# A short block's first product moved behind the full block's first nine products, into another bank, and its copies into other buffers

## The chip, the cores and the metric

The kernel runs on one core of a Trainium2 chip. The metric is the device time of one execution in microseconds (us). An execution holds a linear attention with a recurrent state, a two-layer feed-forward with a leaky activation, and a mixture of eight experts with top-1 routing. The change touches only the experts, the last third of the program.

## The reference, cut to what matters

```python
def _moe2_ref(x, w_gate, w1, w2, capacity):      # x: 1536 x 384, E = 8 experts, F = 1024, capacity 384
    logits = x @ w_gate
    expert_idx = np.argmax(logits, axis=1)
    ...                                          # softmax weight gate_w of the chosen expert
    for i in range(N):                           # tokens go to their expert's list in order
        e = expert_idx[i]
        if counts[e] < capacity:
            disp[e, counts[e]] = x[i]; pos[i] = counts[e]; counts[e] += 1; keep[i] = True
    h = np.maximum(np.einsum('ecd,edf->ecf', disp, w1), 0.0)
    y = np.einsum('ecf,efd->ecd', h, w2)
    for i in range(N):
        if keep[i]: out[i] = gate_w[i] * y[expert_idx[i], pos[i]]
```

With the inputs of these runs the eight experts get 478, 132, 159, 141, 398, 57, 118 and 53 tokens; the first and the fifth are cut to 384.

## The kernel before, in words

Each expert takes its tokens in blocks of 128 rows. The first 128 rows of expert 0 are done earlier, ahead of the loop over experts, so the loop gives expert 0 two full blocks, expert 4 three, and experts 5, 6 and 7 one each. Experts 1, 2 and 3 have more than 128 and at most 160 tokens: they get one full block and a **short block** of up to 32 rows, which is computed beside the full one.

`expert` (line 903) reads the expert's count into a register on every engine (line 1212) and branches (line 923): where the count is marked as "one full and one short", `front(Short(e))` runs, otherwise `front()`. Then, in both cases, the weights of expert e + 2 are loaded through the SP queue (lines 396 and 399 for the two layers, line 654 for the token rows), and `rest()` runs. A further branch (line 934) starts more full blocks where the count asks for them. At the end of a branch that was not taken, each engine brings the semaphores to the values that the branch would have left (the EVENT_SEMAPHORE rows of line 934).

The full block works with split operands (a high and a low part, three products for each true one). `hidden(q, n0, n1)` (line 788) issues products n0 to n1 of the nine that make half q of the hidden layer, into a bank of pool `h`; `relu` (line 793) reads it on ScalarE (ACT); `turn` (line 798) transposes it into a bank of pool `att`, and its second step copies it to `gh` (ACT, line 804) and `gl` (VectorE, line 805). `second` (line 813) multiplies with the second weights into a bank of pool `acc`, and `put` (lines 696, 697) scales the result into `y` on VectorE and scatters its rows to the output with an indirect DMA from GpSimd (POOL). `also(n)` runs work for the next expert beside this one: the casts of its weights on ACT (line 687) with their low parts on VectorE or POOL (line 690), and the transposes of its tokens (line 668).

The short block uses unsplit weights with four groups of 32 rows in parallel: `few.hidden` (`eh_s`, line 869), `few.relu` (`hs_s`, line 875), `few.turn` (`pht_s`, line 881, copied to `hT_s` on VectorE, line 883), `few.second` (`ey_s`, line 892, copied to `part` on ACT, line 896), `few.gather` (`es`, line 900, scaled into `y_s` and scattered).

The order on every engine is the order in which the code is written. Tiles of one tag rotate through the tag's buffers in that order, and also those of branches that are not taken count. PSUM has four banks of pool `acc`, two of `h`, two of `att`. In SBUF the tag `cv` has two buffers: before the change `hs_s`, `hT_s`, `part`, `y` of the first block and `y` of the third share them. Tag `x2T` has one buffer (`y_s`, and `y` of a second block), tag `gl` three.

In `acc` an expert takes eight banks in turn, so `eh_s` of one expert gets the bank in which the expert before had its first block's `ey`, and must wait until VectorE has read that (line 696). In `cv` an expert takes five buffers, so `hT_s` gets the one that held `y` of the expert before, and must wait until its scatter has landed.

Of the kernel before, what the change touches and what calls it, by code (L numbers as in the profile page):

```python
# [8 lines left out]
F32 = mybir.dt.float32  # L9
# [9 lines left out]
P = 128  # L19
# [4 lines left out]
def kernel(  # L24
# [19 lines left out]
    NT, DM = out.shape  # L44
# [17 lines left out]
    HF = F2 // 2  # L62
# [6 lines left out]
    p1 = ctx.enter_context(tc.tile_pool(name="p1", bufs=1))  # L69
    p2 = ctx.enter_context(tc.tile_pool(name="p2", bufs=2))  # L70
    p3 = ctx.enter_context(tc.tile_pool(name="p3", bufs=3))
# [7 lines left out]
    def bank(name, where="att"):  # L79
        pool = {"att": ps_a, "h": ps_h, "acc": ps_acc}[where]  # L80
        return pool.tile([P, 512], F32, tag=where, name=name)
# [202 lines left out]
    def turn(i):  # L284
        t = tiles[i]
        t.turn_r()
        t.turn_k()
# [26 lines left out]
    def finished(i):  # L314
        tiles[i].put_x()


    PHASES = ((ahead, None, (-2, 1, 5, 9)), (turn, turned, (0, 3, 6, 9)), (score0, None, (2, 5, 8, 11)),
              (score1, None, (3, 5, 7, 10)), (output, None, (4, 7, 9, 14)), (finish, finished, (5, 8, 13, 14)))
    ROUTE_AT = ((2, 4, 7, 10, 12, 13, 14),) * (NBLK - 2) + ((2, 3, 4, 5, 6, 7, 8),)  # L320
# [82 lines left out]
    def exp_w(e, q):  # L403
        t = wsl[("e", e, q)]
        c = DC if q < 2 else HF // P
        return [t[:, x * PIECE:(x + 1) * PIECE].rearrange("p (c f) -> p c f", c=c) for x in range(2)]
# [285 lines left out]
    def put(rows, b, acc, name, n=P):  # L692

        pool, tag = ((p2, "cv"), (p1, "x2T"))[b % 2]
        y = pool.tile([P, DM], F32, tag=tag, name=f"y{name}")
        nc.vector.tensor_scalar(y[0:n], acc[0:n], rows[0:n, b, DM:DM + 1], None, op0=ALU.mult)
        ins = nc.gpsimd.indirect_dma_start(out, bass.IndirectOffsetOnAxis(rows[0:n, b, DM + 1:DM + 2].bitcast(I32), 0), y[0:n],  # L697
                                           None, bounds_check=NT - 1, oob_is_err=False)
        for old in puts:
            tc.declare_no_dep(ins.ins, old.ins, reason="each row has one token")  # L700
        puts.append(ins)

    class Early:
# [26 lines left out]
        def hidden(self, q, n0, n1):  # L730
            if n0 == 0:
                self.ph[q] = bank(f"eh_f{q}", "h")
            for n in range(n0, n1):
                (x, y), c = PASS[n // DC], n % DC
                nc.tensor.matmul(self.ph[q], self.d[x][:, c, :], exp_w(0, q)[y][:, c, :],
                                 start=(n == 0), stop=(n == 3 * DC - 1))
# [34 lines left out]
    def expert_block(e, b, beside):  # L771


        nm = f"{e}_{b}"
        d = [t[:, :, b * P:(b + 1) * P] for t in dT[e]]
        ph = [bank(f"eh{nm}_{q}", "h") for q in range(2)]
        h = {0: p2.tile([P, HF], F32, tag="ng", name=f"hs{nm}_0")}
        hT = {0: [p3.tile([P, HF], F32R, tag=t, name=f"{t}{nm}_0") for t in ("gh", "gl")]}

        def also(n):  # L780
            for f in beside.get(n, ()):
                f()

        def hidden(q, n0, n1):
            ww = exp_w(e, q)
            for n in range(n0, n1):
                (x, y), c = PASS[n // DC], n % DC
                nc.tensor.matmul(ph[q], d[x][:, c, :], ww[y][:, c, :], start=(n == 0), stop=(n == 3 * DC - 1))  # L788

        def relu(q):  # L790
            if q not in h:
                h[q] = p2.tile([P, HF], F32, tag="ng", name=f"hs{nm}_{q}")
            nc.scalar.activation(h[q], ph[q], AF.Relu)

        def turn(q):
            pt = bank(f"pht{nm}_{q}")
            for c in range(HF // P):
                nc.tensor.transpose(pt[:, c * P:(c + 1) * P], h[q][:, c * P:(c + 1) * P], ident)  # L798
            if q not in hT:
                hT[q] = [p3.tile([P, HF], F32R, tag=t, name=f"{t}{nm}_{q}") for t in ("gh", "gl")]  # L800
            hh, hl = hT[q]

            def f():
                nc.scalar.copy(hh, pt)  # L804
                nc.vector.tensor_tensor(hl, pt, hh.bitcast(F32), ALU.subtract)  # L805
            return f

        def second(py, q, low, cs=range(HF // P)):
            ww = exp_w(e, 2 + q)
            for c in cs:  # L810
                for x, y in PASS:
                    if (x == 1) == low:
                        nc.tensor.matmul(py, hT[q][x][:, c * P:(c + 1) * P], ww[y][:, c, :],  # L813
                                         start=(q == 0 and not low and c == 0 and y == 0),
                                         stop=(q == 1 and low and c == HF // P - 1))

        def front(few=None):

            if few:
                few.hidden()  # L820
            hidden(0, 0, 3 * DC)
            if few:
                few.relu()
            also(0)
            relu(0)
            if few:
                few.turn()
            hidden(1, 0, 5)
            put_h0 = turn(0)
            if few:  # L830
                few.second()
            also(1)
            put_h0()
            hidden(1, 5, 3 * DC)
            if few:
                few.gather()

        def rest():
            also(2)
            relu(1)  # L840
            also(3)
            py = ps_acc.tile([P, DM], F32, tag="acc", name=f"ey{nm}")
            second(py, 0, False, range(3))
            put_h1 = turn(1)
            put_h1()
            second(py, 0, False, range(3, HF // P))
            second(py, 0, True)
            also(4)
            second(py, 1, False)
            second(py, 1, True)  # L850
            put(dsp[e], b, py, nm)

        return front, rest

    class Short:
# [6 lines left out]
        def hidden(self):  # L862

            n = F2 // NCT
            self.ph = bank(f"eh{self.e}_s", "acc")
            for c in range(DC):
                for j in range(NCT):
                    q, o = j * n // HF, j * n % HF
                    nc.tensor.matmul(self.ph[j * CW:(j + 1) * CW, 0:n], dS[self.e][:, c, :], self.w[q][:, c, o:o + n],
                                     start=(c == 0), stop=(c == DC - 1), skip_group_check=True)  # L870
# [6 lines left out]
        def turn(self):  # L877
            n = F2 // NCT
            pt = bank(f"pht{self.e}_s")
            for c in range(n // P):  # L880
                nc.tensor.transpose(pt[:, c * P:(c + 1) * P], self.h[:, c * P:(c + 1) * P], ident)
            self.hT = p2.tile([P, DM], F32, tag="cv", name=f"hT{self.e}_s")[:, 0:n]
            nc.vector.tensor_copy(self.hT, pt[:, 0:n])

        def second(self):

            n = F2 // NCT // P
            self.pp = bank(f"ey{self.e}_s", "acc")
            for c in range(n):
                for j in range(NCT):  # L890
                    k = j * n + c
                    nc.tensor.matmul(self.pp[j * CW:(j + 1) * CW, 0:DM], self.hT[:, c * P + j * CW:c * P + (j + 1) * CW],
                                     self.w[2 + k * P // HF][:, k % (HF // P), :],
                                     start=(c == 0), stop=(c == n - 1), skip_group_check=True)
            self.part = p2.tile([P, DM], F32, tag="cv", name=f"part{self.e}")
            nc.scalar.copy(self.part, self.pp[:, 0:DM])

        def gather(self):
# [44 lines left out]
    with tc.manual_schedule():  # L943
# [43 lines left out]
        for n in range(7):  # L987
            m = 1 << n
            f = wpow[:, :, n:n + 1].to_broadcast([P, NP, m])
# [168 lines left out]
        g, n = NBLK * NFT - 1, SIZES[-1]  # L1158
# [85 lines left out]
```

## Time and profile before

| what | value |
|---|---|
| three timed runs | 464.07, 465.22, 461.83 us (median 464.07) |
| profiled execution | 462.03 us |
| its span, first to last instruction | 459.9 us |
| mean granted TensorE clock | 0.983 of full speed |
| TensorE (PE) busy | 424.0 us, 92% of the span |
| VectorE, ScalarE, GpSimd busy | 58%, 44%, 35% |
| experts 1, 2, 3 on PE (end of the expert before to own end) | 15.35, 20.15, 16.86 us |

The profile was taken in one execution; times inside it are us from the start of the span. A row of a timeline gives start, duration, engine, line, operation, output and inputs, and in brackets how long the engine was idle before it and what ended that. Rows of the same kind that follow each other are merged (x9). PE rows count each float32 product twice, since it is done in two passes: 12 products of `eh_s` appear as x24. A name with q behind an engine (PEldq, DVEq) is that engine's sequencer, which handles branches and semaphores. The experts lie between 316.9 and 455 us of the span.

### The profile page before, as it was taken

The page shows a single profiled execution, that of the slowest core. Times are in us where ns is not written, and L with a number is a line of the kernel's source. Part 1 is how long each engine was busy: PE and PEld are TensorE (multiplying, and loading weights), DVE is VectorE, ACT ScalarE, POOL GpSimd, SP SyncE. Part 2 cuts the span into 40 slices and gives each one's busy share as a digit, 9 for nine tenths or more (in the row PEclk, how much of TensorE's full clock was granted, in tenths as well). Part 3 has the DMA queues.
Part 4 walks back from the last instruction along what each step waited for, and adds up shares of the span by engine and source line. Part 5 has one row for each costly group of instructions (what it writes and reads, how often), then busy time and mean ns, then how long its engine had stood idle before and what let it go on. Part 6 is the DMA issues. An engine that isn't in the chain of part 4 may idle for free. (4 is left out here: it accounts for less than half of the span.)

```text
span 459.9 us, 7878 instructions
## 1 busy us (share of the span) xinstructions
PE 424.0 (92%) x3012; PEld 363.5 (79%) x3012; DVE 267.9 (58%) x475; ACT 201.7 (44%) x335; POOL 160.0 (35%) x141
## 2 busy tenths in 40 slices
PE   8877989699899999999999999999998887899985
PEld 7765778488788988988898889987966465798774
DVE  6888998999753444345433575354535355443651
ACT  1236545354444333323254444334636366543861
POOL 7845467454440231100300040031407145521660
PEclk9998999989999999999999999999999899899999
DMA  7989950649610105200900020016748728901900
GB/s 130 231 250 280 337 149 3 169 145 358 205 36 17 38 16 201 92 0 6 340 1 1 0 75 12 1 45 192 285 148 281 261 62 298 323 34 41 323 16 19
DMA packets 70513, 62.36 MB, mean 136 GB/s; under 512 B 41837, under 2 KB 58131, under 8 KB 70464
## 3 DMA queue, kind: packets, MB, share of 16 engines
q1 hardware_dynamic: 68832, 57.29, 40.4%
q0 software_dynamic: 1632, 4.40, 2.5%
q8 instruction: 32, 0.52, 0.5%
q14 instruction: 17, 0.14, 0.1%
HBM read 49.99 MB, written 12.18 MB: 135 GB/s over the span
## 5 line engine op out<-in xcount | busy, mean ns | idle before, releaser
L593 PE MATMUL acc<-wm,gh 128*128 128x384 f32 x384 | 100.8, 343 | 0.5 <-POOL wm L372 0.5
L608 PE MATMUL h<-xh,wm 128*128 128x512 f32 (+1 forms) x294 | 87.4, 407 | 3.6 <-DVE gl L631 3.6
L627 DVE SCALAR_TENSOR_TENSOR h<-ng,sign,h 128x512 f32<-128x512 f32 x48 | 36.1, 752 | 67.9 <-ACT ng L624 67.9
L593 PEld LDWEIGHTS acc<-wm,gh 128*128 128x128 f32 x384 | 68.8, 188 | 4.9 <-POOL wm L372 1.1
L593 PE MATMUL acc<-wm,gl 128*128 128x384 f32 x192 | 64.8, 338 | 0.0
L608 PEld LDWEIGHTS h<-xh,wm 128*128 128x128 f32 x294 | 53.2, 192 | 13.3 <-issue 2.9
L788 PE MATMUL eh<-we,d 128*128 128x512 f32 x198 | 54.5, 420 | 5.4 <-ACT we L687 3.1
L690 POOL TENSOR_TENSOR we<-re,we 128x768 fp32r<-128x768 f32 x21 | 41.7, 1984 | 50.8 <-ACT we L687 36.0
L624 ACT ACTIVATE ng<-h,slope 128x512 f32<-128x512 f32 x48 | 33.1, 690 | 57.3 <-PE h L608 57.3
L628 ACT CAST gh<-h 128x512 fp32r<-128x512 f32 x48 | 28.1, 586 | 63.3 <-DVE h L627 63.3
L687 ACT CAST we<-re 128x768 fp32r<-128x768 f32 x64 | 50.6, 839 | 1.8 <-ACTq L934 1.4
L690 DVE TENSOR_TENSOR we<-re,we 128x768 fp32r<-128x768 f32 x43 | 40.7, 973 | 17.8 <-ACT we L687 16.8
L788 PEld LDWEIGHTS eh<-we,d 128*128 128x128 f32 x198 | 37.2, 197 | 17.3 <-issue 9.9
L372 POOL TENSOR_TENSOR wm<-rm,wm 128x768 fp32r<-128x768 f32 x16 | 32.2, 2012 | 46.8 <-ACT wm L371 42.9
L526 POOL DMA_INDIRECT disp<-rows,sl x12 | 12.6, 1048 | 100.0 <-DVE run L552 64.4
L608 PE MATMUL h<-xl,wm 128*128 128x512 f32 (+1 forms) x147 | 42.9, 401 | 0.0
L631 DVE TENSOR_TENSOR gl<-h,gh 128x512 fp32r<-128x512 f32 x48 | 33.0, 687 | 15.6 <-ACT gh L628 15.0
L805 DVE TENSOR_TENSOR gl<-pht,gh 128x512 fp32r<-128x512 f32 x22 | 15.2, 692 | 44.1 <-ACT gh L804 42.4
L813 PE MATMUL ey<-we,gh 128*128 128x384 f32 x176 | 37.7, 346 | 0.0
L593 PEld LDWEIGHTS acc<-wm,gl 128*128 128x128 f32 x192 | 36.1, 188 | 0.0
L608 PEld LDWEIGHTS h<-xl,wm 128*128 128x128 f32 x147 | 28.2, 194 | 6.9 <-DVE xl L274 0.2
L813 PEld LDWEIGHTS ey<-we,gh 128*128 128x128 f32 x176 | 29.7, 189 | 0.4 <-ACT gh L804 0.4
(200 smaller groups left out, 612.8 us busy)
## 6 DMA issues: line engine op xcount, KB each, us to landing
re<-in_moe_w_dram SPq DMA_DIRECT2D x32, 768.0 KB, 6.6
rm<-in_moe_w_in_dram SPq DMA_DIRECT2D x8, 768.0 KB, 5.9
rm<-in_moe_w_out_dram SPq DMA_DIRECT2D x8, 768.0 KB, 6.7
disp<-rowss SPq DMA_DIRECT2D x1, 4825.0 KB
drow<-disp SPq DMA_DIRECT2D x7, 579.0 KB, 8.2
out_dram<-rowss SPq DMA_DIRECT2D x1, 2304.0 KB, 22.7
kn<-in_k_dram SPq DMA_DIRECT2D x10, 192.0 KB, 7.6
rn<-in_r_dram SPq DMA_DIRECT2D x10, 192.0 KB, 3.6
```

The source lines that it names most:

```text
L372: eng.tensor_tensor(lo, low.bitcast(F32), hi.bitcast(F32), ALU.subtract)
L593: nc.tensor.matmul(accs[(blk, s)], gs[g][a][:, s * P:(s + 1) * P], wout[b][:, ft % 2, :], start=(ft == 0 and n == 0), stop=(ft == NFT - 1 ...
L608: nc.tensor.matmul(phs[g][:, cols[0]:cols[1]], win[a][:, c, o:o + P], xs[b][:, c, cols[0]:cols[1]], start=(n == 0), stop=(n == 3 * DC - 1))
L624: nc.scalar.activation(ng, ph, AF.Relu, scale=slope[:, ft:ft + 1])
L627: nc.vector.scalar_tensor_tensor(ph, ng, sign[:, ft:ft + 1], ph, op0=ALU.mult, op1=ALU.add)
L628: nc.scalar.copy(gh, ph)
L631: nc.vector.tensor_tensor(gl, ph, gh.bitcast(F32), ALU.subtract)
L687: nc.scalar.copy(t[:, sl], src[:, sl])
L690: le.tensor_tensor(t[:, sl2], src[:, sl], t[:, sl].bitcast(F32), ALU.subtract)
L788: nc.tensor.matmul(ph[q], d[x][:, c, :], ww[y][:, c, :], start=(n == 0), stop=(n == 3 * DC - 1))
L805: nc.vector.tensor_tensor(hl, pt, hh.bitcast(F32), ALU.subtract)
L813: nc.tensor.matmul(py, hT[q][x][:, c * P:(c + 1) * P], ww[y][:, c, :], start=(q == 0 and not low and c == 0 and y == 0), stop=(q == 1 and ...
```

## The change

In a short expert the full block's first nine products, `also(0)` and the full block's `relu(0)` come first; then the short block's first product and its relu; then five products of the full block's second half; then both transposes. `eh_s` lies in a bank of pool `att` instead of `acc`, `hT_s` in the buffer of tag `x2T` and `part` in a buffer of tag `gl`, both instead of `cv`. The copy to `part` comes behind `also(1)` and the copies of the full block's first half. The branch for experts without a short block keeps its order.

```diff
         def front(few=None):
-            if few:
-                few.hidden()
             hidden(0, 0, 3 * DC)
-            if few:
-                few.relu()
             also(0)
             relu(0)
             if few:
+                few.hidden()
+                few.relu()
+            hidden(1, 0, 5)
+            if few:
                 few.turn()
-            hidden(1, 0, 5)
             put_h0 = turn(0)
             if few:
                 few.second()
             also(1)
             put_h0()
+            if few:
+                few.copy()
             hidden(1, 5, 3 * DC)
             if few:
                 few.gather()
...
-            self.ph = bank(f"eh{self.e}_s", "acc")
+            self.ph = bank(f"eh{self.e}_s")
...
-            self.hT = p2.tile([P, DM], F32, tag="cv", name=f"hT{self.e}_s")[:, 0:n]
+            self.hT = p1.tile([P, DM], F32, tag="x2T", name=f"hT{self.e}_s")[:, 0:n]
...
-            self.part = p2.tile([P, DM], F32, tag="cv", name=f"part{self.e}")
+
+        def copy(self):
+            self.part = p3.tile([P, HF], F32, tag="gl", name=f"part{self.e}")[:, 0:DM]
             nc.scalar.copy(self.part, self.pp[:, 0:DM])
```

On TensorE, at the start of expert 2 (the names end in running numbers; `eh_0_0` and `eh_0_1` are the two halves of the full block's hidden layer):

```order
-L869 MATMUL eh_s<-re_0_3326,ds_3727 32x256 x12
 L788 MATMUL eh_0_0_3924<-we_0_3553,d_2_3551 128x512 x6
 L788 MATMUL eh_0_0_3924<-we_0_3553,d_2_3552 128x512 x3
-L881 MATMUL pht_s<-ident,hs_s 128x128 x2
+L870 MATMUL eh_s<-re_0_3326,ds_3727 32x256 x12
 L788 MATMUL eh_0_1_3925<-we_1_3554,d_2_3551 128x512 x5
+L882 MATMUL pht_s<-ident,hs_s 128x128 x2
 L798 MATMUL pht_0_0_3969<-ident,hs_0_0_3926 128x128 x4
-L892 MATMUL ey_s<-re_2_3329,hT_s 32x384 x8
+L893 MATMUL ey_s<-re_2_3329,hT_s 32x384 x8
```

`eh_s` moved behind nine products of the full block and `pht_s` behind five more; between `pht_s` and `ey_s`, which needs the copy of `pht_s`, five products and four transposes stood before, and now only the four transposes.

On ScalarE, in expert 1 (the same in experts 2 and 3):

```order
-L875 ACTIVATE hs_s<-eh_s 128x256
 L687 CAST we_0_3553<-re_0_3326 128x768 x2
 L793 ACTIVATE hs_0_0_3573<-eh_0_0_3571 128x512
-L896 COPY part_3630<-ey_s 128x384
+L876 ACTIVATE hs_s<-eh_s 128x256
 L687 CAST we_1_3554<-re_0_3326 128x768
 L804 CAST gh_0_0_3574<-pht_0_0_3616 128x512
-L923 UNCONDITIONAL_BRANCH
+L899 COPY part_3634<-ey_s 128x384
```

The casts of the next expert's weights and the full block's relu no longer stand behind `hs_s`, and the cast of the next piece and `gh` no longer behind `part`.

## Rows read from the trace of the kernel before

**Rows 1.** Busy time in three stretches, experts 1, 2 and 3; columns by engine:

```profile
336.68:352.03 15.35, 14.36 (x101) 10.32 (x100) 7.38 (x12) 9.25 (x16) 6.31 (x4) 1.00 0.76 247
352.03:372.18 20.15, 16.10 (x100) 11.06 (x100) 8.79 (x14) 9.74 (x17) 8.04 (x5) 0.92 0.60 208
372.18:389.04 16.86, 14.42 (x100) 10.27 (x100) 8.45 (x14) 9.72 (x17) 8.46 (x5) 1.00 0.69 224
```

**Rows 2.** Timeline of PE, expert 1:

```profile
337.67 1.50 PE L869 MATMUL eh_s<-re,ds 128*32 128x256 f32 x24 [0.99 <-DVEq L934]
339.10 2.37 PE L788 MATMUL eh<-we,d 128*128 128x512 f32 x9
341.31 0.38 PE L881 MATMUL pht_s<-ident,hs_s 128*128 128x128 f32 x2
341.44 1.41 PE L788 MATMUL eh<-we,d 128*128 128x512 f32 x5
342.69 0.60 PE L798 MATMUL pht<-ident,hs 128*128 128x128 f32 x4
343.22 1.50 PE L892 MATMUL ey_s<-re,hT_s 128*32 128x384 f32 x16
344.65 1.20 PE L788 MATMUL eh<-we,d 128*128 128x512 f32 x4
```

**Rows 3.** Timeline of PE, expert 2:

```profile
353.92 1.62 PE L869 MATMUL eh_s<-re,ds 128*32 128x256 f32 x24 [1.89 <-DVEq L934]
...
361.84 2.10 PE L892 MATMUL ey_s<-re,hT_s 128*32 128x384 f32 x16 [2.15 <-DVE hT_s L883]
363.87 2.08 PE L788 MATMUL eh<-we,d 128*128 128x512 f32 x4
```

**Rows 4.** Timeline of PE, expert 3:

```profile
373.84 1.50 PE L869 MATMUL eh_s<-re,ds 128*32 128x256 f32 x24 [1.66 <-DVEq L934]
...
380.24 1.50 PE L892 MATMUL ey_s<-re,hT_s 128*32 128x384 f32 x16 [0.78 <-DVE hT_s L883]
```

**Rows 5.** Timeline of DVE, expert 2:

```profile
353.26 0.61 DVE L696 TENSOR_SCALAR y<-ey,drow 128x384 f32<-128x384 f32 x1
...
361.36 0.42 DVE L883 COPY hT_s<-pht_s 128x256 f32<-128x256 f32 x1 [2.61 <-DMA out_dram<-y,drow]
```

**Rows 6.** Lines 923 and 934, sequencers, 336 to 339 and 352 to 354; min/median/max ns:

```profile
L923 PEldq COMPARE_BRANCH  x1: 81/81/81, 337.5 to 337.5; - x1
L923 PEldq COMPARE_BRANCH  x1: 73/73/73, 352.6 to 352.6; - x1
L934 ACTq EVENT_SEMAPHORE  x1: 17/17/17, 352.5 to 352.5; - x1
L934 DVEq EVENT_SEMAPHORE  x1: 21/21/21, 353.9 to 353.9; - x1
```

**Rows 7.** The same lines, 371 to 374 (start of expert 3):

```profile
L923 PEldq COMPARE_BRANCH  x1: 73/73/73, 372.8 to 372.8; - x1
L934 ACTq EVENT_SEMAPHORE  x1: 17/17/17, 372.7 to 372.7; - x1
```

**Rows 8.** Timeline of POOL, the scatters of experts 0, 1, 1:

```profile
337.62 0.97 POOL L697 DMA_INDIRECT out_dram<-y,drow  x1 [6.64 <-DVEq L934]
...
348.13 1.64 POOL L697 DMA_INDIRECT out_dram<-y_s,drow  x1 [0.16 <-issue]
...
355.17 1.00 POOL L697 DMA_INDIRECT out_dram<-y,drow  x1 [0.16 <-issue]
```

**Rows 9.** DMA packets of the scatters: 339 to 340, 352 to 353, 354 to 355, 360 to 361:

```profile
q0 software_dynamic: 64, 0.20, 52.2%
q0 software_dynamic: 30, 0.01, 3.2%
q0 software_dynamic: 2, 0.00, 0.1%
q0 software_dynamic: 47, 0.12, 29.7%
```

**Rows 10.** Timeline of SP and ACT in experts 1 and 2:

```profile
339.26 0.91 SPq L396 DMA_DIRECT2D re<-in_moe_w_dram  x2
344.82 0.92 SPq L399 DMA_DIRECT2D re<-in_moe_w_dram  x2
...
356.06 1.56 ACT L687 CAST we<-re 128x768 fp32r<-128x768 f32 x2
```

**Rows 11.** Line 923 over the whole span, and PE's first products in experts 4 and 7:

```profile
L923 PEldq COMPARE_BRANCH  x11: 73/183/2307, 316.5 to 444.5; - x11
...
392.12 5.04 PE L788 MATMUL eh<-we,d 128*128 128x512 f32 x14 [3.08 <-ACT we L687]
...
445.03 3.52 PE L788 MATMUL eh<-we,d 128*128 128x512 f32 x14 [1.24 <-ACTq L934]
```

## The prediction

> **What bounds the kernel now.** I first read the busy time of PE over the three stretches in which a short block is computed, experts 1, 2 and 3, each from the end of the expert before to its own end [rows 1]. The three do the same work on PE, yet they last 15.35, 20.15 and 16.86 us. PE is busy 14.36, 16.10 and 14.42 us of that, while VectorE, ScalarE and GpSimd stay under 10 us. So PE bounds these stretches, and two of the three hold something else: idle time of PE (20.15 - 16.10 = 4.05 us in expert 2, 16.86 - 14.42 = 2.44 us in expert 3) and, in expert 2, products that ran slower (16.10 - 14.36 = 1.74 us) at a mean granted clock of 0.92.
>
> Then I read PE's timelines for where the idle time lies. Expert 1 has none behind its first product [rows 2]. In expert 2 it is 1.89 us before `eh_s` and 2.15 us before `ey_s` [rows 3]; 4.04 together, so nothing else is hidden there. In expert 3 it is 1.66 and 0.78 us, the whole 2.44 [rows 4].
>
> Last I read who ends these waits. `eh_s` of expert 2 starts at 353.92; VectorE's `y` (the read of the bank that `eh_s` gets) ran from 353.26 to 353.87 [rows 5], and its sequencer's event of line 934 stands at 353.9, whereas PE's own branch was through at 352.6 + 0.073 = 352.67 [rows 6]. So PE waits for VectorE there, not for the branch. `ey_s` waits for `hT_s`, and `hT_s` waited 2.61 us for a scatter of `y`, until 361.36 [rows 5]: the buffer of tag `cv`. In expert 2 the products behind that wait ran at the lower clock, `ey_s` in 2.10 instead of 1.50 us and the next four in 2.08 instead of 1.20 [rows 2, 3]; that is 1.48 of the 1.74 us, so I count the slowing as a follow-on of the wait.
>
> **The change part by part.**
>
> (a) The start. The first instruction in a short expert is now a full block's product. It needs a bank of pool `h` and operands of the expert before, and a value of ScalarE's counter that stands at 352.5 in expert 2 and 372.7 in expert 3 [rows 6, 7], ahead of PE's branch in both. In expert 1 PE started 0.09 us behind its branch (337.58 to 337.67) [rows 2, 6], so I let it start at 352.76 instead of 353.92 in expert 2, and at 372.8 + 0.07 + 0.09 = 372.96 instead of 373.84 in expert 3 [rows 3, 4, 7]: 1.16 + 0.88 = 2.0 us. In expert 1 the branch itself is last, and nothing is won. The seventh product wants VectorE's low parts; at 2.21 us for nine (339.10 to 341.31 [rows 2]) it comes 1.5 us behind the start, at 354.2, after VectorE's event at 353.9. Even a wait for that event would therefore be over. Bounds: 0 if the wait moves with the first instruction, 2.0 if all goes.
>
> (b) `eh_s` in `att`. It now stands behind nine products (2.2 us) and takes a bank whose last reader was the expert before. Nothing is late there. Its own time is only moved. The short block's relu has a slot while PE does five products (1.25 us, 341.44 to 342.69 [rows 2]).
>
> (c) `hT_s` in `x2T`. The last user of that buffer is `y_s` of the short expert before, scattered far earlier than `y`. For expert 2 the scatter of `y_s` was handed out at 348.13 [rows 8]; its packets moved at 352 to 353, the last two after 354 [rows 9], so it had landed by about 355. With the new start `hT_s` is wanted at 352.76 + 2.2 + 1.45 (`eh_s`, 337.67 to 339.10) + 1.25 + 0.4 = 358.1 [rows 2]: 3 us to spare. In expert 1 the buffer held `y` of expert 0's second block, whose scatter of 337.62 had moved its 64 packets by 340 [rows 8, 9], and `hT_s` comes at 342 or later. So the waits of 2.15 and 0.78 us go, 2.93 us, and with them the slow products, 1.74 + 0.06 = 1.80 us. Bounds: 0 if the scatter of `y_s` is late, 4.7 if it is not.
>
> (d) `part` in `gl`, copied behind a cast and `gh`. `ey_s` takes 1.5 us, and the cast and `gh` (about 0.84 + 0.59) fit beside it; `es` follows four products (1.12 us, 344.65 to 345.77) later. Nothing on the path; if that cover were gone it would be 0.5 us an expert, the length of the copy.
>
> (e) What is closer together now: `pht_s`, then four transposes, then `ey_s`. `pht_s` takes 0.38 us, its copy 0.42 [rows 2, 5], with some 0.1 us of signals; 0.9 in all. PE has 0.13 (341.31 to 341.44) plus 0.53 (342.69 to 343.22) us of work from the start of `pht_s` to `ey_s` [rows 2], where five products more stood in between before. So PE waits about 0.25 us, in three experts: 0.7 us lost. This is the wait that comes next. Bounds: 0, and 0.9 us an expert if the transposes hide nothing.
>
> (f) The queues that are moved past. On ScalarE the casts (1.56 us [rows 10]) now go ahead of `relu(0)`. They start when ScalarE's own branch is through, about 353.1, and are done at 354.7, before PE's nine products end at 355.0. VectorE's low parts then end before 356.6, ahead of `hT_s`. POOL's order is the same, and its first cast comes earlier. SP's load of the first layer of expert e + 2 waits for the last `eh_s` in odd experts (339.26, just behind 339.17) and thus goes out 2.2 us later in the expert; the second load waits for `ey_s` at 344.82 as before [rows 2, 10]. Both share one stretch of traffic, which closes a gap in the traffic and hardly moves its end; the first reader, the casts at 356.06, moves to 353.1. Cost 0, and some 2 us if the load were late there.
>
> **Sum.** 2.0 + 2.93 + 1.80 - 0.7 = 6.0 us. From the end of expert 3 on, the same work follows on PE, so I carry all of it to the end. The profiled execution took 462.03 us, 2.1 more than its span, and becomes 456.0. The three timed runs have a median of 464.07, and the mean of the four executions is 463.3; I take that middle: 463.3 - 6.0 = **457.3 us**. Runs differ by 3 us, so 1% (4.6 us) is about what can be told from no change; 459.4 is where "faster" begins.
>
> **The rivals.**
>
> - *The start is not won* (chance 0.12). The first product's wait covers more than it needs and still ends with VectorE's event. For it: in the branch not taken, PE's first products in expert 7 came 1.24 us behind the last product [rows 11]. Against: there PE's own branch explains it. Gain 6.0 - 2.0 = 4.0: 459.3.
>
> - *The wait goes from one scatter to another* (0.13). The scatter of `y` was handed out at 355.17 and landed at 361.36, 6.2 us, its packets moving at 360 among the weights' load [rows 5, 8, 9]. If that of `y_s`, whose last two packets came after 354, slips into the same load, `hT_s` of expert 2 waits to 361.3 again, and start and stall of expert 2 bring nothing: 6.0 - 1.16 - 2.15 - 1.74 = 1.0, so 462.3. The Trainium skill ("DMA: Bandwidth & Descriptors", Queues, rings and completion order) says that a DMA engine serves its queues in turn, packet by packet; by that, a small scatter is never held up behind a load, this rival falls, and the sum stays at 6.0. The trace does not agree: a scatter in an idle stretch was through in under 2.6 us and this one took 6.2.
>
> - *Slower: the jump* (0.06). In expert 4, the first without a short block after three with one, PE's branch took 2.307 us where the eleven have a median of 0.183, and PE's 14 products then took 5.04 instead of 3.52 us [rows 11]: 2.1 + 1.5 = 3.6 us. Experts 0, 5, 6 and 7 jump to the same kind of place and paid nothing. If the new code is laid out so that they pay too, each costs 3.6; the second one eats the gain, and with all four it is 457.3 + 14.4 = 471.7. Against: the instructions on PE are as many as before. The Trainium skill ("Runtime: NRT & Kernel Launch", Instruction fetch mechanics) says that a taken branch whose target is not in the stretch already fetched waits for a fetch by DMA; by that rule where pages end decides, and one expert can pay and the next not, as here.
>
> - *The jump of expert 4 becomes cheap* (0.09), by the same layout: 457.3 - 3.6 = 453.7.
>
> The forecast itself has 0.60. **Range:** 453.5 to 462.3, from the cheap jump to the scatter in place of the scatter; beyond it lie the slow jumps and half of the tails. **Chances:** faster by over 1%: 0.50 of the forecast's 0.60 (its bounds and the spread of runs take the rest), half of the first rival, and the cheap jump, 0.65. Slower by over 1% (above 468.7): 0.05, the jumps. Within 1%: 0.30.
>
> **What would show it.** (a): PE's gap before the first product of experts 2 and 3 falls from 1.89 and 1.66 to about 0.75. (c): `hT_s` without a DMA behind its wait, the clock of expert 2's stretch at 1.00, `ey_s` at 1.50 us. (e): a gap of 0.2 to 0.3 us before `ey_s` in all three. All together: stretches of 15.4 to 15.6 us for experts 1, 2 and 3. I am wrong if `hT_s` still waits for a scatter, if the first product still starts at VectorE's event, or if PE's branch takes over 2 us in more experts than one.

## The result, and the profile after

The change takes the kernel from a median of 464.1 us (12 runs) to 459.17 us (12 runs). The medians lie 4.93 us apart and the means 4.08 us (463.35 and 459.27); the ratio, which goes by all runs and not by the two medians, is 0.9913, 95% interval 0.9892 to 0.9933. The profiled execution took 457.6 us with a span of 455.8; that of before 462.03 with 459.9. Every profile below is of one execution, and what is read from it holds for that one.

Busy time in four stretches of the changed kernel: experts 1, 2 and 3, each from the end of the expert before to its own end, and the rest. Columns as in [rows 1]: length, busy us and count of PE, PEld, DVE, ACT and POOL, granted clock, DMA share, GB/s.

```profile
336.40:352.07 15.67, 14.61 (x100) 10.24 (x100) 7.56 (x12) 9.44 (x16) 5.56 (x4) 1.00 0.68 233
352.07:367.49 15.42, 14.61 (x101) 10.24 (x100) 8.91 (x14) 9.94 (x17) 8.41 (x5) 1.00 0.82 280
367.49:382.92 15.43, 14.62 (x101) 10.24 (x100) 8.93 (x14) 9.95 (x17) 8.29 (x5) 1.00 0.67 229
382.92:455.80 72.88, 60.16 (x321) 53.12 (x321) 31.02 (x46) 35.19 (x56) 27.72 (x17) 0.98 0.36 127
```

And the rest in the kernel before, from the end of expert 3 on:

```profile
389.04:459.90 70.86, 60.15 (x322) 53.12 (x321) 31.25 (x46) 35.19 (x56) 27.97 (x17) 0.96 0.37 127
```

The three stretches are now alike, at full clock, and last 46.52 us together instead of 52.36 [rows 1]: 5.84 us less. But the rest lasts 72.88 instead of 70.86 us, with the same busy time of PE: 2.02 us more. With 0.28 us that the execution happened to be ahead at the start of expert 1 (336.40 against 336.68), 0.28 + 5.84 - 2.02 = 4.10 us, the difference of the spans.

PE's timeline of the changed kernel, expert 2 [rows 3 for before]:

```profile
352.80 2.35 PE L788 MATMUL eh<-we,d 128*128 128x512 f32 x9 [0.73 <-ACTq L937]
355.08 1.50 PE L870 MATMUL eh_s<-re,ds 128*32 128x256 f32 x24
356.51 1.43 PE L788 MATMUL eh<-we,d 128*128 128x512 f32 x5
357.79 0.38 PE L882 MATMUL pht_s<-ident,hs_s 128*128 128x128 f32 x2
358.00 0.60 PE L798 MATMUL pht<-ident,hs 128*128 128x128 f32 x4
358.68 1.50 PE L893 MATMUL ey_s<-re,hT_s 128*32 128x384 f32 x16
360.11 1.19 PE L788 MATMUL eh<-we,d 128*128 128x512 f32 x4
...
368.22 2.36 PE L788 MATMUL eh<-we,d 128*128 128x512 f32 x9 [0.72 <-ACTq L937]
```

The first row starts 0.73 us behind the expert before, and the timeline shows no gap behind it. The last row is the start of expert 3. VectorE's copy in expert 2 [rows 5 for before] now waits for PE alone:

```profile
358.20 0.42 DVE L884 COPY hT_s<-pht_s 128x256 f32<-128x256 f32 x1 [1.65 <-PE pht_s L882]
```

Where the 2.02 us went, PE's timeline shows at its first products of experts 4 and 6 [rows 11 for before, expert 4]:

```profile
386.79 5.05 PE L788 MATMUL eh<-we,d 128*128 128x512 f32 x14 [3.88 <-issue]
...
429.51 3.51 PE L788 MATMUL eh<-we,d 128*128 128x512 f32 x14 [2.26 <-PEq L937]
```

Before, these gaps were 3.08 and 1.04 us:

```profile
433.62 3.52 PE L788 MATMUL eh<-we,d 128*128 128x512 f32 x14 [1.04 <-ACTq L934]
```

0.80 + 1.22 = 2.02 us. The branches of PE's sequencer beside them, changed kernel (min/median/max ns, start):

```profile
L926 PEldq COMPARE_BRANCH  x1: 3047/3047/3047, 383.6 to 383.6; - x1
L937 PEldq COMPARE_BRANCH  x1: 2940/2940/2940, 425.6 to 425.6; - x1
```

The first is the branch into expert 4, which took 2.307 us before; the second jumps over the further blocks at the end of expert 5, and before it took 0.333 us (two branches of line 934 of the kernel before, out of experts 4 and 5):

```profile
L934 PEldq COMPARE_BRANCH  x2: 187/260/333, 420.9 to 430.9; - x2
```

So the question for the experiments was double: which of the three parts (order, bank, buffers) brought the 5.84 us, and why branches that the change doesn't touch got dearer. The code cuts of `e1_bank`, `e2_buffers` and `e6_before_pad64` are against the kernel before, the others against the change; each ratio is against executions of the kernel before that were run beside it.

### The profile page after: what moved, and what is told of

Its sections match the earlier page's. It is cut to its first block, busy times and chain, and to the rows that moved or that the text cites. A ratio compares the mean times of both kernels' runs of the same rounds, so it can differ in the third digit from the quotient of the medians.

```text
span 455.8 us, 7866 instructions
## 1 busy us (share of the span) xinstructions
PE 420.9 (92%) x3012; PEld 361.2 (79%) x3012; DVE 267.6 (59%) x475; ACT 202.5 (44%) x335; POOL 160.1 (35%) x141
```

## The experiments

**Bank alone** (`e1_bank`): the old order and buffers.

```diff
-            self.ph = bank(f"eh{self.e}_s", "acc")
+            self.ph = bank(f"eh{self.e}_s")
```

> The kernel before with one line of the change: eh_s in a bank of pool att; order and buffers as before. Theory A (eh_s waited for its bank, the one that y reads): the gaps before eh_s fall from 1.89 and 1.66 to about 0.75 us in experts 2 and 3; in expert 2 the copy hT_s still waits for the scatter of y until the same moment, so only expert 3 can gain, and that too only until its own scatter: total 0 to 1 us. Theory B (the bank in att was last used in a block that was not run, so the wait is for VectorE's counter, which stands only behind y): the gaps stay at 1.9 and 1.7 us, time as before (464).

Measured: 465.21 us, ratio 1.0059 (1.0027 to 1.0091). The starts of experts 2 and 3 in its PE timeline:

```profile
354.66 1.50 PE L869 MATMUL eh_s<-re,ds 128*32 128x256 f32 x24 [2.00 <-DVEq L934]
...
373.32 1.50 PE L869 MATMUL eh_s<-re,ds 128*32 128x256 f32 x24 [1.77 <-DVEq L934]
```

The gaps did not fall, they grew by 0.1 us. Theory A falls, and theory B fits: by the order of allocation in the code the bank in `att` was last used in a block that is not run, and the row that ends the wait is VectorE's event behind `y`. The bank by itself gains nothing. That the time rose by 0.6% instead fits the branch out of expert 5, which this one line already made dear:

```profile
L934 PEldq COMPARE_BRANCH  x1: 3093/3093/3093, 430.7 to 430.7; - x1
```

Before expert 6 the gap was 2.41 us here, 1.04 in the kernel before.

**Buffers alone** (`e2_buffers`): old order and bank; `hT_s` in `x2T`, `part` in `gl`, its copy behind `gh` as in the change (that call is not shown).

```diff
-            self.hT = p2.tile([P, DM], F32, tag="cv", name=f"hT{self.e}_s")[:, 0:n]
+            self.hT = p1.tile([P, DM], F32, tag="x2T", name=f"hT{self.e}_s")[:, 0:n]
...
-            self.part = p2.tile([P, DM], F32, tag="cv", name=f"part{self.e}")
+        def copy(self):
+            self.part = p3.tile([P, HF], F32, tag="gl", name=f"part{self.e}")[:, 0:DM]
```

> The kernel before with the other part of the change alone: hT_s in x2T, part in gl (its copy behind gh, as in the change), order and bank as before. If the scatter's buffer was the wait: hT_s of experts 2 and 3 has no DMA behind it, the 2.15 and 0.78 us before ey_s and the slow products go, no gap before ey_s in any expert; the gaps before eh_s stay at 1.9 and 1.7 us. Stretches of experts 1, 2, 3: 15.35, 16.3, 16.1 us; 4.7 us less than before in them, about 459.4 in all if the jumps stay as before. Rival (the wait goes to the scatter of y_s): the stretch of expert 2 stays near 20 us.

Measured: 458.79 us, ratio 0.9924 (0.9891 to 0.9957). Its three stretches:

```profile
338.38:353.73 15.35, 14.36 (x101) 10.32 (x100) 7.48 (x12) 9.34 (x16) 5.55 (x4) 1.00 0.74 245
353.73:369.74 16.01, 14.35 (x100) 10.27 (x100) 8.46 (x14) 9.83 (x17) 7.82 (x5) 1.00 0.76 264
369.74:385.77 16.03, 14.37 (x101) 10.28 (x100) 8.47 (x14) 9.84 (x17) 7.71 (x5) 1.00 0.70 239
```

No wait before `ey_s`, full clock, gaps of 1.66 us before `eh_s` in experts 2 and 3: 47.39 us, 4.97 less than before (expected 4.7). The branch out of expert 5 stayed cheap here (0.34 us, a gap of 0.97 us before expert 6). The buffers alone thus bring as much as the whole change, within what these runs can tell. In the three stretches the whole change is 0.87 us better (46.52), but it pays 1.29 us more before expert 6.

**All but the order** (`e3_old_order`): buffers and bank, `eh_s` first as before.

```diff
+            if few:
+                few.hidden()
             hidden(0, 0, 3 * DC)
+            if few:
+                few.relu()
             also(0)
             relu(0)
             if few:
-                few.hidden()
-                few.relu()
-            hidden(1, 0, 5)
-            if few:
                 few.turn()
+            hidden(1, 0, 5)
```

> All of the change but the order: bank att, hT_s in x2T, part in gl, eh_s first as before. Theory A (the bank was the wait): gaps before eh_s of 0.75 us, no gap before ey_s: stretches of 15.35, 15.1, 15.1 us, 0.9 us less than the change. Theory B (the counter): gaps of 1.9 and 1.7 us as in e2, so the order is what makes the bank usable: stretches as in e2, 16.3 and 16.1.

Measured: 460.43 us, ratio 0.9956 (0.9928 to 0.9984).

```profile
355.48 1.50 PE L871 MATMUL eh_s<-re,ds 128*32 128x256 f32 x24 [1.77 <-DVEq L938]
...
371.61 1.50 PE L871 MATMUL eh_s<-re,ds 128*32 128x256 f32 x24 [1.77 <-DVEq L938]
```

Gaps before `eh_s` of 1.77 us in experts 2 and 3, none before `ey_s`: theory B again, 0.1 us above `e2_buffers` in both. The order is what brings the starts forward, since the wait for VectorE's event then lies behind 2.2 us of other products: with it the three stretches last 46.52 instead of 47.72 us. Whether the new order needs the new bank at all was not tried.

**Order and bank alone** (`e4_cv`): the change with `hT_s` and `part` back in `cv`.

```diff
-            self.hT = p1.tile([P, DM], F32, tag="x2T", name=f"hT{self.e}_s")[:, 0:n]
+            self.hT = p2.tile([P, DM], F32, tag="cv", name=f"hT{self.e}_s")[:, 0:n]
...
-            self.part = p3.tile([P, HF], F32, tag="gl", name=f"part{self.e}")[:, 0:DM]
+            self.part = p2.tile([P, DM], F32, tag="cv", name=f"part{self.e}")
```

> The change with hT_s and part back in cv: order and bank of the change alone. The first products start at 0.75 us, but hT_s waits for the scatter of y: in expert 2 wanted at 358.1 and free at about 361.3, 3.2 us of wait instead of 2.15 and the lower clock behind it, stretch about 20 us as before; in expert 3 the wait grows from 0.78 to about 1.7. Time as before within 1 us. Rival (the start is worth its 2 us by itself): 2 us less than before.

Measured: 466.33 us, ratio 1.0064 (1.0026 to 1.0103). PE, experts 2 and 3:

```profile
356.31 2.36 PE L788 MATMUL eh<-we,d 128*128 128x512 f32 x9 [0.73 <-ACTq L937]
...
365.84 1.90 PE L893 MATMUL ey_s<-re,hT_s 128*32 128x384 f32 x16 [3.72 <-DVE hT_s L884]
...
383.22 1.50 PE L893 MATMUL ey_s<-re,hT_s 128*32 128x384 f32 x16 [0.52 <-DVE hT_s L884]
```

The start is won and waited away again: 3.72 us in expert 2 (3.2 expected), with the clock falling behind it. In expert 3 I expected 1.7 and it was 0.52; the scatter landed earlier there, for a reason that I did not follow up. Nor did the time stay within 1 us: it rose by 0.64%. In the profile the gap before expert 6 is 2.28 us (branch out of expert 5: 2.96 us) instead of 1.04, and the one before expert 4 is 3.42 us with 5.99 us of products behind it, instead of 3.08 and 5.04. Without the buffers the order gains nothing.

**Code further on, work the same** (`e5_pad32`, `e5_pad64`, `e5_pad96`): products are issued again in expert 0's third block, which is not run with these inputs. (The first product opens its sum anew each time, so the block's result would be the same.)

```diff
-            for n in range(n0, n1):
+            for n in [0] * (32 if (e, b, q) == (0, 2, 0) and n0 == 0 else 0) + list(range(n0, n1)):
```

> The change with 32 products more (64 instructions) in the code of PE, in expert 0's third block, which isn't run with these inputs: the code behind it lies further on, the work done is the same. Theory layout (where the code's pieces that are fetched together end decides which jump pays): PE's branches that took 3.05 us (into expert 4) and 2.94 us (out of expert 5) change, each to below 0.5 us or to another jump; the stretches of experts 1 to 3 stay at 15.4 us. Theory traffic (a jump pays because the weights' load fills the DMA engines then): both stay at 2.3 to 3.0 us.

> The same with 64 products (128 instructions). Layout: another set of jumps pays than with 0 and 32; each paid jump that goes is worth 1.2 us (out of expert 5) to 3.6 us (into expert 4, with the lower clock behind it). Traffic: as the change.

> The same with 96 products (192 instructions). Layout: a third set; with some of the three pads the branch out of expert 5 is below 0.5 us again. Traffic: as the change.

**No load beside the branch** (`e7_no_load7`): expert 7's weights are not loaded, and it computes with expert 5's.

```diff
                 for q in range(NPIECE):
-                load_expert(e + 2, q)
+                if e + 2 == 7:
+                    raws[("e", 7, q)] = raws[("e", 5, q)]
+                else:
+                    load_expert(e + 2, q)
```

> The change without the load of expert 7's weights (expert 7 then computes with expert 5's, so its rows are others): no weights move while PE jumps out of expert 5. Theory traffic: that branch falls from 2.94 to below 0.5 us. Theory layout: it still pays a fetch, shortened at most by what the load held it up, so 1.5 to 2.5 us; the branch into expert 4 stays at 2.3 to 3.0 in both.

**The kernel before with the same padding** (`e6_before_pad64`):

> The kernel before with 64 products more in the code that isn't run. Layout: with nothing else altered other jumps pay, as with the same pad in the change (4.0, 4.5 and 1.1 us there), and the time rises by 3 to 6 us, to 467 to 470. Traffic: as before (464).

The branches of PE in the profiled executions of all these, in us, and the time against the kernel before:

| kernel | out of exp. 1 | out of 3 | into 4 | out of 5 | into 6 | into 7 | ratio (95% interval) |
|---|---|---|---|---|---|---|---|
| before | 0.22 | 0.34 | 2.31 | 0.33 | 0.21 | 0.33 | 1 |
| the change | 0.22 | 0.35 | 3.05 | 2.94 | 0.22 | 0.42 | 0.9913 (0.9892 to 0.9933) |
| the change, pad 32 | 1.55 | 0.34 | 2.93 | 0.32 | 0.22 | 0.22 | 0.9862 (0.9816 to 0.9908) |
| the change, pad 64 | 1.18 | 4.04 | 0.23 | 0.33 | 4.46 | 1.10 | 0.9986 (0.9957 to 1.0015) |
| the change, pad 96 | 0.34 | 1.11 | 0.23 | 0.22 | 1.68 | 1.68 | 0.9856 (0.9802 to 0.9910) |
| no load of expert 7 | 0.22 | 0.35 | 3.01 | 1.40 | 0.22 | 0.42 | 0.9840 (0.9805 to 0.9876) |
| before, pad 64 | 0.34 | 3.57 | 0.22 | 0.33 | 3.17 | 1.57 | 1.0162 (1.0113 to 1.0210) |

Layout decides **which** branch pays: the padding does no work, and with each another set pays, though with 32 products the branch into expert 4 stayed dear, which the layout theory did not expect. The edit itself moves code too: the trace of the kernel before has 86 EVENT_SEMAPHORE rows on PE's sequencer, those of the change and of `e1_bank`, `e3_old_order` and `e4_cv` have 83, and these four pay out of expert 5 (2.44 to 3.09 us); `e2_buffers` has 79 and does not. The same padding of 64 makes the branches out of expert 3 and into 6 and 7 dear in both kernels, and takes the kernel before to 469.92 us, slower by 1.6% for code that never runs. In the change it eats the whole gain. There the first products of experts 4, 6 and 7 show both costs, the gap and the clock:

```profile
386.69 6.09 PE L788 MATMUL eh<-we,d 128*128 128x512 f32 x14 [3.37 <-PEq L937]
...
433.41 5.03 PE L788 MATMUL eh<-we,d 128*128 128x512 f32 x14 [5.21 <-issue]
...
446.92 5.04 PE L788 MATMUL eh<-we,d 128*128 128x512 f32 x14 [1.86 <-issue]
```

What a branch waits for, the instruction queue shows. Without the load the branch out of expert 5 took 1.40 us instead of 2.94, neither below 0.5 as the traffic theory had it nor quite the 1.5 us of the layout theory, and the next expert started with a gap of 0.98 us. It ran from 427.69 to 429.09. From 426 to 429, counted by their start, the DMA queues of that execution held the end of a small load and one packet of the instruction queue, which moved from 426.76 to 427.73:

```profile
q1 hardware_dynamic: 131, 0.18, 16.1%
q8 instruction: 1, 0.02, 2.0%
```

In the change the same branch ran from 425.57 to 428.51, and the packet moved among the load, from 426.09 to 427.11 (queues from 425 to 429):

```profile
q1 hardware_dynamic: 1030, 1.54, 104.0%
q8 instruction: 1, 0.02, 1.6%
```

That branch waits for a fetch of code: both times it ended 1.4 us behind the end of the packet. The same holds in all traces: of the 31 branches of PE that took over 0.5 us in the 14 traces, each ended 1.36 to 1.53 us behind the end of such a packet of 16 KB, which itself took 0.93 to 1.40 us.

What sets **how much** a branch pays is when its packet starts: 0.93 us ahead of the branch without the load, 0.52 us behind its start in the change. The packet is not slower beside the load (1.02 against 0.97 us); it comes later. For this branch the load is thus the likely cause of the difference, by one execution without it. It is not the rule for all: with 64 products of padding the branch out of expert 1 took 1.18 us beside 380 GB/s. Why the branch into expert 4 took 2.65 to 3.49 us in the kernels with the new order, where it paid, and 2.05 to 2.55 in those with the old one is open.

1.40 us hides behind products that PE still has queued, 2.94 us does not. The Trainium skill ("Runtime: NRT & Kernel Launch", Instruction fetch mechanics) says that a taken branch whose target lies outside the code at hand waits for a fetch by DMA. The traces agree, with the packets just named. They also show a wait without a branch. With 32 products of padding PE stopped between the seventh and the eighth product of expert 6, and went on 1.53 us behind the end of a packet at 431.28:

```profile
432.81 1.79 PE L788 MATMUL eh<-we,d 128*128 128x512 f32 x7 [0.86 <-issue]
```

**Transposes earlier** (`e8_turn3`, `e8_turn3_pad32`, `e8_turn3_pad96`): the change with `pht_s` behind three of the five products, without and with padding.

```diff
-            hidden(1, 0, 5)
+            hidden(1, 0, 3)
             if few:
                 few.turn()
+            hidden(1, 3, 5)
             put_h0 = turn(0)
```

> The change with pht_s two products earlier: behind three of the five products instead of all five, so that two products and four transposes stand between it and ey_s. The 0.3 us by which the stretches of the change exceed 14.36 us of products fall to about 0.1: stretches of 15.1 to 15.2 us, 0.6 us less in the three. In the total that shows only if the same jumps pay as in the change (then 458.5); where they pay otherwise, the jumps decide by up to 4 us.

> The same with 32 products more in the code that isn't run. Layout: the branch out of expert 5 below 0.5 us as in the change with this pad; about 457.8 to 458.0. Traffic alone: 2.9 us there.

> The same with 96 products more. Layout: the branch into expert 4 below 0.5 us, those into experts 6 and 7 about 1.7 us, as in the change with this pad; about 457.6. The fastest of these three would be the fastest kernel here.

Measured: 459.75 us and 0.9925 (0.9897 to 0.9954); 458.99 and 0.9918 (0.9886 to 0.9950); 456.5 and 0.9865 (0.9827 to 0.9903). PE, expert 2 of the first:

```profile
355.33 2.36 PE L788 MATMUL eh<-we,d 128*128 128x512 f32 x9 [0.73 <-ACTq L938]
...
360.55 0.60 PE L798 MATMUL pht<-ident,hs 128*128 128x128 f32 x4
361.08 1.50 PE L894 MATMUL ey_s<-re,hT_s 128*32 128x384 f32 x16
```

From `pht` to `ey_s` it is 0.53 us as before, instead of 0.68, and from the start of `eh` to `ey_s` 5.75 instead of 5.88: 0.13 us an expert (0.2 expected), too little to be seen in the times. What shows there is the set of branches again. Without padding the same two pay as in the change (3.31 and 2.96 us). With 32 the branch out of expert 5 took 0.32 us as expected, the one into expert 4 3.49 us, and the time was 1 us above the expected 458. With 96 the branch into expert 4 took 0.23 us and those into 6 and 7 took 0.74 and 1.52. That last kernel had the lowest median and the lowest single run, 454.1 us; the change with 96 and with 32 products of padding can't be told from it.

## Why the prediction was right, and where it was not

- **(a) The start.** Right: the gaps fell from 1.89 and 1.66 to 0.73 and 0.72 us, 2.10 us (2.0 forecast), and nothing in expert 1. The reason was not complete: I gave the new bank and the new order one credit. `e1_bank` and `e3_old_order` show that the bank without the order leaves the wait where it was.
- **(b)** Right: `eh_s` never waits behind the nine products.
- **(c) The buffers.** Right: 2.15 + 0.78 us of waits gone, and with them 1.80 us of slow products; the clock of expert 2's stretch is 1.00. `e2_buffers` gives 4.97 us for it, 4.7 forecast. The rival that one scatter's wait takes the place of another did not come: `hT_s` has no DMA behind it.
- **(d)** Right: PE does not wait for `part`.
- **(e)** Right in kind, larger than forecast, and not where I looked: the first product to the end takes 14.69 us (337.38 to 352.07 in expert 1) instead of 14.36, so 0.33 us an expert and 1.0 in all, where I had 0.7. PE's weight loads for `ey_s` do wait 0.9 us for `hT_s` in the three experts, but the gap of 0.2 to 0.3 us before `ey_s` that was to show it is not in the timeline: `pht` to `ey_s` takes 0.68 instead of 0.53. `pht_s` to what follows takes 0.21 instead of 0.13, and the nine products 2.29 instead of 2.21 us. In `e8_turn3` no weight load waits for `hT_s` any more, and only 0.13 of the 0.33 us came back; where the other 0.2 come from is not shown.
- **(f)** Right for the casts and the loads: no stretch waits for them. What I missed shows in the sum.
- **The sum** was 6.0 us in the three stretches and is 2.10 + 2.93 + 1.80 - 1.0 = 5.83, measured 5.84. The step that failed is the one behind it, "I carry all of it to the end". 2.02 us were given back at the branches into expert 4 and out of expert 5. In the rival of the jumps I had the mechanism and the place of one of the two, but argued against it with the number of instructions on PE. That it is as many as before was wrong (83 semaphore rows instead of 86), and no argument either: the padded kernels show that the place of the code counts. And I let only jumps into an expert pay, not the one out of an expert. One of my own signs of being wrong thus came: PE's branch took over 2 us in two places (3.05 and 2.94). 457.3 was forecast, 459.17 came. That is the number of the first rival (459.3), but not its cause: the starts were won.
- **Chances.** 0.65 on more than 1% was too much. I took the forecast from the mean of 463.3 and the mark of 1% (459.4) from the median of 464.07; from the same mean it is 458.7, nearer to the forecast. The ratio came out just under it, at 0.87% (the medians alone at 1.06%), and the two branches are the difference.

## What to carry to other kernels

A buffer or bank that rotates by program order is followed to its last user in that order, also where that user is a block that is not run: what stands in for it may be the latest event of the whole branch, and a new bank then moves no wait, while an order that puts other work in front hides it. Where a program branches at run time, compare the branch times of the sequencer in both traces before the difference is put down to the edit: code that moved by a few instructions can change the total by as much as the edit. A padding in code that is not run helps to tell the two apart.

## What the runs showed of the hardware that I had not expected

A branch of PE's sequencer took between 0.07 and 4.46 us in these executions. Each that took over 0.5 us ended 1.36 to 1.53 us behind the end of a 16 KB packet of the instruction queue, so its price goes by how early that packet starts: 1.40 us where it started 0.93 us ahead of the branch, 4.46 us where it started 1.92 us behind its start (with 64 products of padding, into expert 6). Behind the idle time that it makes the clock can be halved as well: behind the gap of 3.88 us before expert 4 the granted clock fell from 2.4 to 1.2 GHz and fourteen products took 5.05 us instead of 3.51. The length of the gap alone does not decide it: behind the 2.26 us before expert 6 they took 3.51 us, behind 1.86 us before expert 7 with 64 products of padding 5.04.
